# Attention and a gated feed-forward on one core: the eight PSUM banks become one pool, buffers are placed by the plan, and the order is another

## The chip, the cores and the metric

One core of a Trainium2 chip runs the whole program. TensorE (PE) multiplies matrices out of SBUF into the eight banks of PSUM; VectorE (DVE), ScalarE (ACT) and GpSimd (POOL) do the rest, the first two out of SBUF and PSUM, the third out of SBUF alone in this kernel; SyncE (SP) issues the DMAs. The metric is the device time of one execution in microseconds, the median over the runs. A measurement of this kernel tells a difference of about 0.2% from none.

## What is computed

```
# q, k, v: (8 batches, 8 heads, 576 positions, 64); attention inside chunks of 64 positions
scores = scale * q_c @ k_c.T                    # per batch, head and chunk: 64 x 64
attn   = exp(scores - max) ; attn /= sum + 1e-9
x      = attn @ v_c  -> (8, 576, 512)           # heads side by side
h      = relu(x @ w_in)                         # 512 -> 1024
c[s]   = w0*h[s-1] + w1*h[s] + w2*h[s+1]        # depthwise, along the positions of a batch
out    = (h * sigmoid(c)) @ w_out               # 1024 -> 512
```

q, k and v are fp32. The three weights arrive in 64-bit words, which the kernel reads as pairs of 32-bit words and turns into fp32 itself.

## The kernel before

**Tiles and blocks.** The 4608 positions of all batches are 36 tiles of 128 (two chunks of 64 each). Four tiles are one unit `u` (9 units of 512 columns). For each tile: q and k are loaded and turned (`t_pe` on PE and a copy out of PSUM for tiles 0 to 8, `t_dve` on DVE from tile 9), `scores` on PE (16 products of 64x64 per head half, 32 in all), the softmax (`s_max`, `s_sub` on DVE, `s_exp` on ACT, `s_sum`, `s_eps`, `s_rec` on DVE, a scaling on POOL), the transpose of the weights (`p_pe` on PE for tiles 0 to 11, later a swap by DMA and `p_dve`), `attn_v` on PE, and the result split into a high and a low part (`x_hi` on ACT, `x_lo` on DVE). From tile 4 on two tiles go through scores and attention together.

**The feed-forward.** Every product with a weight is three matmuls (high by high, high by low, low by high). `mm1` makes one block of 128 of the 1024 features for one unit: 12 matmuls of 512 columns (for unit 0 two halves of 256, since its first two tiles are there earlier). ACT and DVE then work on the block in its PSUM bank: `h_relu`, copies of the rim columns, `c_mid`, `c_left`, `c_right`, `c_sig`, `c_mul`; the bank is held from `mm1` to the end of `c_mul`. `g_hi` (on ACT, DVE or POOL) and `g_lo` (POOL) split the result. `mm2` then sums 8 features x 3 matmuls for one output tile of 128 rows into one bank, `o_copy` takes it out (ACT or DVE) and `o_store` writes it.

**The weights.** Each piece is loaded (`w_load`), scaled on ACT (`w_scale`), put together on DVE (`w_shift`, `w_words`) and split (`w_hi`, `w_left`, on the engine that the table `moved_` names).

**PSUM before.** Six banks (`banks`, index chosen by the plan) serve everything but scores and attention; these two share one pair of banks, `sx`: each tile uses one half (256 columns) of both banks, so two tiles fill the pair. Scores of the next two tiles can't begin before `x_lo` of the last attention has read the pair, and attention not before `s_sub` of the last scores.

**SBUF before.** Working buffers come from pools that rotate by the order of allocation (`rawv`, `work`, `work3`).

**The order.** All work is cut into 1990 steps, each with its engine, a planned cost, what it waits for, and what buffers it takes and frees. A list, `order_`, gives the sequence that was found by a search outside the kernel; `moved_` gives the engine of the steps that have a choice. The kernel runs through `order_` once, keeps a clock for each engine, hands out banks (each time the one that is free longest), and then emits the steps in order of their planned start. Each engine keeps that order. Where the plan leaves PE idle in its first 110 us, filler matmuls on the identity are put in (L978 of 512 columns, L981 of 128); their result isn't used.

Of the kernel before, what the change touches and what calls it, by code (L numbers as in the profile page):

```python
# [18 lines left out]
def attn_ffn(ctx: ExitStack, tc: tile.TileContext, q, k, v, w_in, conv_w, w_out, out):  # L19
# [4 lines left out]
    P = 128  # L24
# [14 lines left out]
    NB = 6  # L39
# [4 lines left out]
    rawv = ctx.enter_context(tc.tile_pool(name="rawv", bufs=3))  # L44
    work = ctx.enter_context(tc.tile_pool(name="work", bufs=2))
    work3 = ctx.enter_context(tc.tile_pool(name="work3", bufs=3))
    sb_w, sb_g = ExitStack(), ExitStack()
    ps_s = ctx.enter_context(tc.tile_pool(name="ps_s", bufs=1, space=PSUM))
    ps_b = ctx.enter_context(tc.tile_pool(name="ps_b", bufs=1, space=PSUM))
# [12 lines left out]

    sx = [ps_s.tile([P, 2, 512], F32, name=f"sx{i}_ps") for i in range(4 - NB // 2)]
    banks = [None] * NB
# [57 lines left out]
    def load_group(j):  # L122

        if not groups:
            sb_w.close()
            groups["raw"] = ctx.enter_context(tc.tile_pool(name="raw", bufs=2, side="right"))
        groups[j] = groups["raw"].tile([P, 2, G, 4 * TG, 32], F32, name="qk")
# [17 lines left out]
    def load_v(st, t):  # L145
# [6 lines left out]
        r = rawv.tile([P, G, 2, D], F32, name="v")  # L152
# [5 lines left out]
        if t == 0:  # L158
            st["u"] = work3.tile([P, UN], F32, name="c")[:, 0:G * D].rearrange("p (g d) -> p g d", d=D)
            heads(st["u"], 0, 1, slice(1, H, 2), C)  # L160
        else:
            st["u"] = st["last"]["w"]
# [18 lines left out]
    def turned(st):  # L181
        if 0 not in st:
            st["qk"] = work.tile([P, 2, G, 2 * C], F32, name="qkT")
            st[0], st[1] = st["qk"][:, 0], st["qk"][:, 1]
        return st["qk"]
# [15 lines left out]
    def sx_half(i):  # L201
        return sx[i // 2][:, :, G * C * (i % 2):G * C * (i % 2) + G * C]

    def sx_bank(i, u):
        return sx_half(i)[:, u, :]

    def scores(st):

        qT, kT = st[0], st[1]
        for g in range(G):  # L210
            for s in range(2):
                for hp in range(2):
                    d0 = 64 * hp
                    nc.tensor.matmul(  # L214
                        sx_bank(st["s"], hp if st["t"] >= TP else hp ^ s)[C * s:C * s + C, C * g:C * g + C],
# [5 lines left out]
    def s_max(st):  # L221
        st["m"] = work.tile([P, 2, G], F32, name="m")
        sv = sx_half(st["s"]).rearrange("p u (g j) -> p u g j", j=C)
        nc.vector.tensor_reduce(out=st["m"], in_=sv, op=ALU.max, axis=AX.X)  # L224

    def s_sub(st):
        st["e"] = work.tile([P, H, C], F32, name="e")
        nc.vector.tensor_tensor(
            out=st["e"].rearrange("p (g u) j -> p u g j", u=2), in0=sx_half(st["s"]).rearrange("p u (g j) -> p u g j", j=C),
# [9 lines left out]
    def s_sum(st):  # L239
        st["z"] = work.tile([P, H], F32, name="z")  # L240
# [11 lines left out]
    def two(st, name):  # L252
        if name not in st["two"]:
            st["two"][name] = work3.tile([P, 2 * DM], F32, name="wt").rearrange("p (n b h j) -> p n b h j", n=2, b=2, h=H)
        return st["two"][name][:, st["n"]]
# [15 lines left out]
    def p_dve(st):  # L271
        st["pT"] = work.tile([P, G, P], F32, name="pT")
# [13 lines left out]
    def p_copy(st, copy=nc.scalar.copy):  # L286
        st["pT"] = work.tile([P, G, P], F32, name="pT")
# [5 lines left out]
    def attn_v(st):  # L293
        for g in range(G):
            for s in range(2):
                for hp in range(2):
                    j0, m, vt = C * s, hp, st["v"][:, :, hp, :]
                    if st["t"] < TP:
# [4 lines left out]
                        sx_bank(st["x"], s)[D * hp:D * hp + D, C * g:C * g + C],  # L303
# [17 lines left out]
    def x_src(st):  # L321
        return sx_half(st["x"]).rearrange("p s (g i) -> p g s i", i=C)
# [46 lines left out]
    def c_mid(st, u, f):  # L369
        i0, n = span(u)  # L370
        st["c"] = work3.tile([P, UN], F32, name="c")[:, 0:n]
# [99 lines left out]
    def o_copy(st):  # L471
        st["os"] = work.tile([P, DM], F32, name="os")
        nc.scalar.mul(out=st["os"], in_=banks[st["o"]], mul=0.5)

    def o_copy_v(st):
        st["os"] = work.tile([P, DM], F32, name="os")
# [12 lines left out]
    def w_load(st, src):  # L489
        np_, n, m2 = src.shape  # L490
        if "at" not in st and "wslot" not in st:
            t = work.tile([P, DM], F32, name="os")
# [8 lines left out]
    def w_tile(st, name):  # L501
        n = st["L"].shape[1] * st["L"].shape[2]
        if name == "wt":
            st["w"] = work3.tile([P, 2 * DM], F32, name="wt")
# [81 lines left out]
    room = {"slot": 2, "wslot": 2, "sx": 8 - NB, "bk": NB, "grp": 2, "v": 3, "qkT": 2, "m": 2, "e": 2, "z": 2, "pT": 2, "c": 3, "wt": 3, "os": 2, "rc": 2}  # L586
    slot_users, place_users, row_users = [], {}, []

    def split(key, t_load, src, hi=None, lo=None, half=False, at=None):
# [4 lines left out]
        ld = step("SP", 0.57, t_load, w_load, (st, src), take=["os"] if small else [("wslot", st)] if at is None else [], lag=0.1 if small else 2.7 if at == 0 else 1.5 if half else 3.0)  # L594
        if small:
            s1 = step("DVE", a, key, w_mask, (st,), [ld], take=["wt"], port=True)
# [3 lines left out]
            s5 = step("DVE", b, key + 0.03, w_sign, (st,), [s2, s4], free=["os"], port=True)  # L600
# [3 lines left out]
            s8 = step("PE", 0.2, key + 0.04, c_pe, (st,), [s8], take=[("bk", st, "ct")], free=["wt"])  # L604
            return step("DVE", 0.2, key + 0.04, c_copy, (st,), [s8], free=[("bk", "ct")])
        s1 = step("ACT", c + 0.09, key, w_scale, (st,), [ld], take=["wt"])
        s2 = step("DVE", a, key, w_shift, (st,), [s1], port=True)
        s4 = step("DVE", b, key + 0.01, w_words, (st,), [s2], free=["wslot"] if at is None else [], port=True)
# [419 lines left out]
```

## Time and profile before

| | |
|---|---|
| median of 3 runs | 486.23 us (485.35 to 486.42) |
| profiled execution: its time / its span | 483.82 us / 482.0 us |
| PE busy | 469.7 us (97%) |
| DVE / ACT / POOL busy | 347.7 (72%) / 231.3 (48%) / 191.4 us (40%) |
| granted clock of PE, mean | 0.998 |
| HBM read / written | 36.72 / 9.44 MB |

The span runs from the first to the last instruction; the 1.8 us between the span and the execution's own time lie around it. The profiled execution is 2.4 us shorter than the median of the three runs. A matmul's busy time includes its pipeline, so matmuls in a row overlap in the records; what a stretch takes is read from starts.

### The profile page before, as it was taken

What the parts mean: (1) busy time and instruction counts of PE and PEld (TensorE: products, weight loads), DVE (VectorE), ACT (ScalarE), POOL (GpSimd) and SP (SyncE); (2) the same over time, 40 slices, a digit from 0 to 9 for tenths busy, and PEclk for the clock granted to TensorE, in tenths of its full rate; (3) what the DMA queues carried; (4) which work ended last, traced back from release to release, by engine and by line L of the source; (5) the groups of instructions that cost most, each with busy time, mean ns of one, the idle gap of its engine ahead of it and who ended that gap; (6) DMA issues with size and microseconds to landing.
All of it is one profiled execution on the core that took longest, in us unless ns stands there. A gap on an engine that the chain in (4) does not pass through costs nothing.

```text
span 482.0 us, 11324 instructions
## 1 busy us (share of the span) xinstructions
PE 469.7 (97%) x4401; PEld 386.2 (80%) x4401; DVE 347.7 (72%) x612; ACT 231.3 (48%) x531; POOL 191.4 (40%) x257
## 2 busy tenths in 40 slices
PE   8889999999999999999999999999999999999996
PEld 6789878887888888888888888888788888888885
DVE  3899997778758883989389748785779488624640
ACT  3547873555454742473267336651544165423430
POOL 1435546143333561355145423543255415502330
PEclk9999999999999999999999999999999999999999
DMA  7999945334567454336464624236642014000102
GB/s 213 234 303 248 274 68 95 67 51 78 96 149 176 97 99 116 49 72 134 110 139 76 123 67 106 48 56 158 117 92 46 22 63 114 3 22 22 45 22 87
DMA packets 180457, 50.06 MB, mean 104 GB/s; under 512 B 164508, under 2 KB 172724, under 8 KB 180404
## 3 DMA queue, kind: packets, MB, share of 16 engines
q1 hardware_dynamic: 180404, 49.34, 45.2%
q8 instruction: 34, 0.56, 0.5%
q14 instruction: 19, 0.16, 0.1%
HBM read 36.72 MB, written 9.44 MB: 96 GB/s over the span
## 4 chain that ended last, share of the span: by engine, by line
PE 75%; SPq 12%; DVE 7%; issue 2%; DMA 2%; POOL 1%; ACT 1%; POOLq 0%; ACTq 0%; DVEq 0%
PE b_ps L468 36%; PE b_ps L336 31%; SPq L141 10%; PE sx_ps L302 3%; PE sx_ps L214 3%; DMA r<-in_k 2%; DVE wt L520 1%; DVE wt L515 1%; SPq L111 1%; PE b_ps L174 1%; DVE x_l L328 1%; PE b_ps L283 1%; SPq L150 1%; DVE c L377 1%; DVE m L224 0%
## 5 line engine op out<-in xcount | busy, mean ns | idle before, releaser
L416 POOL TENSOR_TENSOR g_l<-c,g_h 128x510 fp32r<-128x510 f32 (+1 forms) x80 | 79.6, 1003 | 105.2 <-DVE g_h L405 43.4
L468 PE MATMUL b_ps<-wo_h,g_h 128*128 128x512 f32 x288 | 114.9, 399 | 1.0 <-ACT qkT L192 1.0
L468 PE MATMUL b_ps<-wo_h,g_l 128*128 128x512 f32 x288 | 112.3, 390 | 0.0
L468 PE MATMUL b_ps<-wo_l,g_h 128*128 128x512 f32 x288 | 112.2, 390 | 0.0
L336 PE MATMUL b_ps<-x_h,wi_h 128*128 128x512 f32 (+1 forms) x320 | 80.7, 374 | 0.0
L377 DVE SCALAR_TENSOR_TENSOR c<-b_ps,cw,c 128x510 f32<-128x510 f32 x72 | 53.1, 740 | 36.8 <-ACT rim L362 17.5
L336 PE MATMUL b_ps<-x_l,wi_h 128*128 128x512 f32 (+1 forms) x320 | 78.8, 368 | 0.0
L336 PE MATMUL b_ps<-x_h,wi_l 128*128 128x512 f32 (+1 forms) x320 | 78.7, 368 | 0.0
L343 ACT ACTIVATE b_ps<-b_ps 128x512 f32<-128x512 f32 x62 | 36.2, 584 | 73.2 <-PE b_ps L336 73.0
L336 PEld LDWEIGHTS b_ps<-x_l,wi_h 128*128 128x128 f32 x320 | 56.8, 188 | 10.2
L336 PEld LDWEIGHTS b_ps<-x_h,wi_l 128*128 128x128 f32 x320 | 56.9, 188 | 10.0
L468 PEld LDWEIGHTS b_ps<-wo_h,g_h 128*128 128x128 f32 x288 | 54.0, 188 | 13.4 <-issue 1.3
L336 PEld LDWEIGHTS b_ps<-x_h,wi_h 128*128 128x128 f32 x320 | 55.9, 188 | 10.5 <-DVE c L393 0.2
L468 PEld LDWEIGHTS b_ps<-wo_h,g_l 128*128 128x128 f32 x288 | 54.1, 188 | 11.5
L468 PEld LDWEIGHTS b_ps<-wo_l,g_h 128*128 128x128 f32 x288 | 54.1, 188 | 10.3
L389 ACT ACTIVATE c<-c 128x510 f32<-128x510 f32 (+1 forms) x72 | 45.4, 634 | 31.8 <-DVE c L383 31.3
L372 ACT ACTIVATE c<-b_ps,cw 128x510 f32<-128x510 f32 (+1 forms) x72 | 49.7, 692 | 21.6 <-DVE b_ps L347 15.6
L393 DVE SCALAR_TENSOR_TENSOR c<-c,b_ps 128x510 f32<-128x510 f32 (+1 forms) x72 | 48.1, 671 | 10.2 <-ACT c L389 6.6
L383 DVE SCALAR_TENSOR_TENSOR c<-b_ps,cw,c 128x510 f32<-128x510 f32 (+1 forms) x72 | 53.4, 744 | 2.2 <-ACT rim L362 0.7
L405 POOL CAST g_h<-c 128x510 fp32r<-128x510 f32 x25 | 15.3, 611 | 69.0 <-DVE c L393 68.2
L259 POOL TENSOR_TENSOR wt<-wt,z 128x512 f32<-128x512 f32 x24 | 25.2, 1052 | 42.1 <-DVE z L250 21.3
L199 DVE STREAM_TRANSPOSE qkT<-qk 128x512 f32<-128x512 f32 x54 | 36.2, 687 | 6.6 <-DMA qk<-in_k 4.2
(87 smaller groups left out, 518.8 us busy)
## 6 DMA issues: line engine op xcount, KB each, us to landing
out<-os SPq DMA_DIRECT2D x35, 256.0 KB, 2.3
v<-in_v SPq DMA_DIRECT2D x21, 256.0 KB, 3.6
qk<-in_k SPq DMA_DIRECT2D x96, 48.0 KB, 2.4
qk<-in_q SPq DMA_DIRECT2D x96, 48.0 KB, 2.4
w<-in_moe_w_out SPq DMA_DIRECT2D x4, 1024.0 KB, 5.3
v<-in_v SPq DMA_DIRECT2D x27, 128.0 KB, 3.1
wt<-wt SPq DMA_DIRECT2D x48, 64.0 KB, 2.0
qk<-in_k SPq DMA_DIRECT2D x96, 24.0 KB, 1.9
```

The source lines that it names most:

```text
L141: nc.sync.dma_start(out=groups[j][p0:p0 + 32, i, g, n0:n0 + 2 * n, :], in_=(q, k)[i][b, 2 * g + hp, t0:t0 + C * n, 32 * a:32 * a + 32].rea ...
L199: nc.vector.transpose(out=turned(st)[:, i].rearrange("p g (n i) -> p g n i", i=32), in_=groups[t // TG][:, i, :, 4 * (t % TG):4 * (t % TG) ...
L259: nc.gpsimd.tensor_tensor(out=two(st, "to"), in0=two(st, "of"), in1=z, op=ALU.mult)
L336: nc.tensor.matmul(banks[st["h"]][:, c0:c1], lhsT=wt[:, f // 2, kt, P * (f % 2):P * (f % 2) + P], rhs=xt[:, u % 2, kt, c0:c1], start=n == ...
L343: nc.scalar.activation(out=h, in_=h, func=AF.Relu)
L372: nc.scalar.mul(out=st["c"], in_=banks[st["h"]][:, i0:i0 + n], mul=cw[:, FT + f:FT + f + 1])
L377: nc.vector.scalar_tensor_tensor(out=c[:, a:n], in0=banks[st["h"]][:, i0 + a - 1:i0 + n - 1], scalar=cw[:, f:f + 1], in1=c[:, a:n], op0=AL ...
L383: nc.vector.scalar_tensor_tensor(out=st["c"], in0=banks[st["h"]][:, i0 + 1:i0 + 1 + n], scalar=cw[:, 2 * FT + f:2 * FT + f + 1], in1=st["c ...
L389: nc.scalar.activation(out=st["c"], in_=st["c"], func=AF.Tanh, scale=0.5)
L393: nc.vector.scalar_tensor_tensor(out=st["c"], in0=st["c"], scalar=1.0, in1=banks[st["h"]][:, i0:i0 + n], op0=ALU.add, op1=ALU.mult)
L416: nc.gpsimd.tensor_tensor(out=g_l[:, f, gs], in0=st["c"][:, cs], in1=g_h[:, f, gs].bitcast(F32), op=ALU.subtract)
L468: nc.tensor.matmul(banks[st["o"]], lhsT=gt[:, f, o:o + P], rhs=wt[:, f, :], start=f == 0 and n == 0, stop=f == FT - 1 and n == 2)
```

## The change

- The pair `sx` is gone. One PSUM tile `b_ps` of eight banks serves all. Scores or attention of two tiles take two neighbouring banks when they begin and give them back when the last `s_sub` or `x_lo` has read them. `bank_for` chooses: among banks that are free in time, those with the fewest open neighbours.
- The rotating pools are replaced by fixed tiles (`spots`); the plan says which of them a step uses. Numbers of buffers are the same (`room`).
- Steps that read one bank on ACT and DVE (the rim copies and `c_left`/`c_right`, and now each visit by itself) are kept apart in the plan by a tag (`bank=`).
- `order_` and `moved_` are new, from a search under two models of the loads.

```
-    NB = 6
+    NB = 8
...
-    sx = [ps_s.tile([P, 2, 512], F32, name=f"sx{i}_ps") for i in range(4 - NB // 2)]
-    banks = [None] * NB
+    room = {"slot": 2, "wslot": 2, "bk": NB, "grp": 2, "v": 3, "qkT": 2, "m": 2, "e": 2, "z": 2, "pT": 2, "c": 3, "wt": 3, "os": 2, "rc": 2}
...
+    all_banks = ps_s.tile([P, NB, 512], F32, name="b_ps")
+    banks = [all_banks[:, i] for i in range(NB)]
...
+    def half(st, name):
+
+        b, o = st["both"][name, 0], G * C * st["half"]
+        return all_banks[:, b:b + 2, o:o + G * C]
...
-                 take=[("sx", st_, "s") for st_ in sts], free=["qkT"] * len(tiles), bank="sx")
+                 take=[("bk", both, ("s", u)) for u in range(2)], free=[("qkT", st_["t"]) for st_ in sts], bank=tag)
...
-                 take=[("sx", st_, "x") for st_ in sts], bank="sx",
+                 take=[("bk", both, ("x", u)) for u in range(2)], bank=tag + 1, behind=[before.get("attn")],
...
-    moved_ = {15: 1, 16: 0, 21: 1, 27: 1, 28: 0, 33: 1, 39: 0, 45: 1, 51: 1, 58: 0, 64: 0, 69: 1, 73: 0, 94: 0,
+    moved_ = {16: 0, 22: 0, 27: 1, 34: 0, 40: 0, 45: 1, 46: 0, 51: 1, 63: 1, 70: 0, 73: 0, 94: 0, 113: 0, 132: 0,
...
+    bank_free = [0.0] * NB
+
+    def bank_for(t, n, late_):
+
+        best = None
+        for b in range(NB + 1 - n):
+            if any(x is None for x in bank_free[b:b + n]):
+                continue
+            since = max(bank_free[b:b + n])
+            open_ = (b > 0 and bank_free[b - 1] is not None) + (b + n < NB and bank_free[b + n] is not None)
+            rank = (0, open_, since if n == 1 else 0.0) if since + late_ <= t else (1, since, 0.0)
+            if best is None or rank < best[0]:
+                best = rank, b
+        return best[1]
```

What the new order moves, at three places. First PE just ahead of the first `mm2`, before (L336 is `mm1`, L214 scores, L179 the turning of q and k, L468 `mm2`, L978 and L981 fillers):

```order
L981 MATMUL b_ps<-ident 128x128 x3
L214 MATMUL sx_ps<-qkT 64x64 x32
L336 MATMUL b_ps<-x_h,wi_h 128x256 x4
L336 MATMUL b_ps<-x_l,wi_h 128x256 x4
L336 MATMUL b_ps<-x_h,wi_l 128x256 x4
L978 MATMUL b_ps<-ident 128x512
L981 MATMUL b_ps<-ident 128x128 x6
L179 MATMUL b_ps<-ident,qk_107 128x128 x8
L468 MATMUL b_ps<-wo_h,g_h 128x512
```

and the same place now, from the scores of tiles 6 and 7 (L220) on; L289 is `p_pe`, L342 `mm1`:

```order
L220 MATMUL b_ps<-qkT_72 64x64 x16
L220 MATMUL b_ps<-qkT_73 64x64 x16
L289 MATMUL b_ps<-ident,e_76 128x128 x4
L342 MATMUL b_ps<-x_h,wi_h 128x256 x4
L342 MATMUL b_ps<-x_l,wi_h 128x256 x4
L342 MATMUL b_ps<-x_h,wi_l 128x256 x4
```

The fillers on either side of these scores are gone, and the scores stand before the attention of tiles 4 and 5 instead of behind it. After the first load PE has 20 fillers of 128 columns and one of 512 before, 6 and one now. All of unit 0's `mm1` now stands ahead of the first `mm2`; before, 2 of its 16 halves stood behind. Ahead of the first `mm1` of unit 1 stand 18 steps of `mm2` (3 matmuls each) before and 6 now.

Second PE in the long even part, before: attention (L302) and, further on, scores (L214) each stand alone between products of the feed-forward:

```order
L336 MATMUL b_ps<-x_h,wi_h 128x512 x4
L336 MATMUL b_ps<-x_l,wi_h 128x512 x4
L336 MATMUL b_ps<-x_h,wi_l 128x512 x4
L302 MATMUL sx_ps<-pT,v 64x64 x32
L468 MATMUL b_ps<-wo_h,g_h 128x512
```

and now attention (L308) with the scores (L220) of other tiles right behind it:

```order
L342 MATMUL b_ps<-x_h,wi_l 128x512 x4
L308 MATMUL b_ps<-pT_80,v_69 64x64 x16
L308 MATMUL b_ps<-pT_81,v_67 64x64 x16
L220 MATMUL b_ps<-qkT_72 64x64 x16
L220 MATMUL b_ps<-qkT_73 64x64 x16
L474 MATMUL b_ps<-wo_h,g_h 128x512
```

Attention and scores of two tiles stand side by side at 9 places behind the first `mm1` of unit 1 now (4 times attention first, 5 times scores), at none before; the total of matmuls but for the fillers is the same.

Third the stores at the end of SP's queue, before (the last output tile is written in three pieces):

```order
L486 DMA out<-os 128x512 x10
L482 DMA out<-os 112x512
L483 DMA out<-os 15x512
L484 DMA out<-os 1x512
```

and now, where the tile in three pieces is the last but one:

```order
L488 DMA out<-os_71 112x512
L489 DMA out<-os_71 15x512
L490 DMA out<-os_71 1x512
L492 DMA out<-os_70 128x512
```

The last copy out of PSUM was on DVE and is on ACT now. On DVE, ahead of the eighth `c_mul` of unit 0, the new order has fewer instructions (110 for 120): no `g_hi` (6 before), no `p_copy` (1), 4 copies of turned q and k for 7, no cast of a weight (1), and one `w_left` of 512 columns more.

## Rows read from the trace of the kernel before

**Rows 1.** Busy time by stage: PE, its loads, DVE, ACT, POOL, PE's clock, DMA share.
```profile
0.00:5.24 5.24, 3.78 (x11) 2.27 (x11) 0.00 (x0) 1.49 (x2) 1.37 (x8) 1.00 0.45 126
5.24:62.45 57.21, 50.77 (x855) 45.55 (x856) 51.29 (x90) 35.86 (x66) 23.52 (x22) 1.00 0.98 258
62.45:71.49 9.04, 8.93 (x111) 7.22 (x111) 8.63 (x19) 6.29 (x12) 4.72 (x7) 1.00 0.43 70
71.49:478.00 406.51, 406.22 (x3432) 331.16 (x3425) 287.06 (x503) 187.71 (x454) 161.79 (x222) 1.00 0.39 82
478.00:482.00 4.00, 0.00 (x0) 0.00 (x0) 0.69 (x1) 0.00 (x0) 0.00 (x0) 0.76 0.37 131
```
**Rows 2.** PE's waits: line, releaser, us in total, times, longest.
```profile
PE b_ps L283 <- POOL e L276: 2.6, 4, 1.0
PE b_ps L174 <- DMA r<-in_k: 1.7, 2, 1.4
PE b_ps L468 <- ACT qkT L192: 1.0, 1, 1.0
PE sx_ps L214 <- DVE x_l L328: 0.9, 2, 0.7
```
**Rows 3.** Groups of PE between 5.24 and 71.49 us: the fillers.
```profile
L981 PE MATMUL b_ps<-ident 128*128 128x128 f32 x20 | 3.3, 278 | 0.0
L978 PE MATMUL b_ps<-ident 128*128 128x512 f32 x2 | 1.0, 590 | 0.0
```
**Rows 4.** PE in order of time around the first `mm2`: start, us.
```profile
55.02 0.49 PE L981 MATMUL b_ps<-ident 128*128 128x128 f32 x3
56.24 1.16 PE L214 MATMUL sx_ps<-qkT 64*64 64x64 f32 x64 [0.74 <-DVE x_l L328]
...
58.86 1.02 PE L978 MATMUL b_ps<-ident 128*128 128x512 f32 x2
59.72 0.82 PE L981 MATMUL b_ps<-ident 128*128 128x128 f32 x6
60.37 1.04 PE L179 MATMUL b_ps<-ident,qk 128*128 128x128 f32 x8
62.45 0.47 PE L468 MATMUL b_ps<-wo_h,g_h 128*128 128x512 f32 x1 [1.04 <-ACT qkT L192]
...
80.47 1.07 PE L336 MATMUL b_ps<-x_h,wi_h 128*128 128x512 f32 x4
```
**Rows 5.** The chain of waits, 159.98 to 174.40 us: start, us.
```profile
162.92 2.72 PE b_ps L336 x12
165.64 1.09 PE sx_ps L302 x64
166.73 2.95 PE b_ps L468 x12
169.68 1.09 PE sx_ps L214 x64
170.77 0.90 PE b_ps L468 x3
171.67 2.73 PE b_ps L336 x12
174.40 0.68 PE b_ps L468 x3
```
**Rows 6.** Groups of DVE over the span, by form.
```profile
L405 DVE CAST g_h<-c 128x127 fp32r<-128x127 f32 x4 | 1.8, 443 | 0.1
L405 DVE CAST g_h<-c 128x384 fp32r<-128x384 f32 x4 | 1.4, 348 | 0.0
L288 DVE COPY pT<-b_ps 128x512 f32<-128x512 f32 x3 | 2.0, 675 | 0.2 <-PE b_ps L283 0.2
L192 DVE COPY qkT<-b_ps 128x512 f32<-128x512 f32 x2 | 1.4, 683 | 0.0
L559 DVE CAST wi_h<-wt 128x1024 fp32r<-128x1024 f32 x1 | 0.7, 683 | 0.0
L524 DVE TENSOR_TENSOR wi_l<-wt,wi_h 128x512 fp32r<-128x512 f32 x2 | 1.4, 688 | 0.5 <-POOL wi_h L562 0.5
```
**Rows 7.** All engines at the end, in order of time: start, us.
```profile
477.38 0.60 ACT L473 ACTIVATE os<-b_ps 128x512 f32<-128x512 f32 x1 [6.83 <-PE b_ps L468]
477.58 0.39 PE L468 MATMUL b_ps<-wo_h,g_l 128*128 128x512 f32 x1
...
478.01 0.69 DVE L477 TENSOR_SCALAR os<-b_ps 128x512 f32<-128x512 f32 x1 [8.83 <-PE b_ps L468]
478.72 0.35 SPq L482 DMA_DIRECT2D out<-os  x1
479.13 0.45 SPq L483 DMA_DIRECT2D out<-os  x1
479.63 0.24 SPq L484 DMA_DIRECT2D out<-os  x1
```
**Rows 8.** The page's DMA issues: count, KB each, us to landing.
```profile
out<-os SPq DMA_DIRECT2D x35, 256.0 KB, 2.3
```

More of the change, by code (lines that the diff above doesn't have):

```diff
@@ L239, in s_sum @@
     def s_sum(st):
-        st["z"] = work.tile([P, H], F32, name="z")
+        st["z"] = spot("z", st["t"])
         if st["t"] >= TP:
@@ L491, in w_load @@
         if "at" not in st and "wslot" not in st:
-            t = work.tile([P, DM], F32, name="os")
+            t = spot("os", id(st))
         else:
@@ L630, in att @@
             ld = group(t // TG)
-            tt = [step("DVE", 0.7, key - 3, t_dve, (st, t, i), ld, take=["qkT"] * (1 - i)) for i in range(2)]
+            tt = [step("DVE", 0.7, key - 3, t_dve, (st, t, i), ld, take=[("qkT", t)] * (1 - i)) for i in range(2)]
             tt[1]["after"].append(tt[0])
             if t % TG == TG - 1:
-                tt[1]["free"] = ["grp"]
+                tt[1]["free"] = [("grp", t // TG)]
         parts = 1 if (2 * t) % NCK < NCK - 1 else 2
@@ L657, in attend @@
+        before["attn"] = s
         for st_ in sts:
             t = st_["t"]
-            a = step("ACT", 0.58, key + 1, x_hi, (st_, t), [s] + writes, bank="sx")
-            x_done[t] = step("DVE", 0.69, key + 1, x_lo, (st_, t), [a], free=[("sx", "x")], bank="sx")
-    def soft(st, s, key):
-        s = step("DVE", 0.69, key, s_max, (st,), [s], take=["m"], bank="sx")
-        s = step("DVE", 0.68, key, s_sub, (st,), [s], take=["e"], free=["m", ("sx", "s")], bank="sx")
+            a = step("ACT", 0.58, key + 1, x_hi, (st_, t), [s] + writes, bank=tag + 1)
+            x_done[t] = step("DVE", 0.69, key + 1, x_lo, (st_, t), [a], behind=[x_done[t - 1] if st_ is not sts[0] else None],
+                             free=[("bk", both, ("x", u)) for u in range(2)] if st_ is sts[-1] else [], bank=tag + 1)
@@ L665, in soft @@
+    def soft(st, s, key, tag, last):
+        s = step("DVE", 0.69, key, s_max, (st,), [s], take=[("m", st["t"])], bank=tag)
+        s = step("DVE", 0.68, key, s_sub, (st,), [s], take=[("e", st["t"])], behind=[st["both"].get("sub")],
+                 free=[("m", st["t"])] + [("bk", st["both"], ("s", u)) for u in range(2)] * last, bank=tag)
+        st["both"]["sub"] = s
         fold = st["t"] >= TP
         first = fold and not st["n"]
-        s = step("ACT", 0.63, key + 1, s_exp, (st,), [s], behind=[fold and st["two"].get("exp")], take=["wt"] * first, free=["e"] * fold)
+        s = step("ACT", 0.63, key + 1, s_exp, (st,), [s], behind=[fold and st["two"].get("exp")], take=[("wt", "of", st["t"])] * first, free=[("e", st["t"])] * fold)
@@ L668, in soft @@
         st.get("two", {})["exp"] = s
-        s = step("DVE", 0.68, key + 2, s_sum, (st,), [s], take=["z"])
+        s = step("DVE", 0.68, key + 2, s_sum, (st,), [s], take=[("z", st["t"])])
         s = step("DVE", 0.17, key + 2, s_eps, (st,), [s], port=True)
@@ L725, in rim_steps @@
         st = {}
-        s = step("POOL", 0.25, key, r_mid, (st, u), rims[u - 1] + rims[u], take=["rc"], port=True)
+        s = step("POOL", 0.25, key, r_mid, (st, u), rims[u - 1] + rims[u], take=[("rc", u)], port=True)
         for k in (0, 2):
@@ L961, in attn_ffn @@
         free_at[e] = t + cost - early[e]
-        for r in s["free"]:
-            r, name = (r, r) if isinstance(r, str) else r
-            b = s["args"][0][name] if r in ("slot", "wslot", "sx", "bk") else held[r][0]
-            held[r].remove(b)
-            free_buf[r].append((end[i], b))
+        for r, *who in s["free"]:
+            b = home_of[(r, *(id(x) if isinstance(x, dict) else x for x in who))]
             if r == "bk":
-                taken[b][-1][1] = end[i]
-    for i in range(NB):
-        banks[i] = ps_b.tile([P, 512], F32, name=f"b{i}_ps")
+                bank_free[b] = taken[b][-1][1] = end[i]
+            else:
+                free_buf[r].append((end[i], b))
     made = {}
```

168 lines of the change are left out of this document (92 added, 76 removed), and 211 rows, old and new, of tables (moved_, order_).

## Prediction, made before the changed kernel ran

> **What bounds the kernel now.** I read the busy times by stage first, because a PE that is busy 97% of the span says little while its fillers count as work. The table [rows 1] cuts the span at five places: the first real product (5.24 us), the first `mm2` (62.45), the end of the attention of tiles 6 and 7 (71.49) and the last product (478.0). Three things are to be seen. From 71.49 us on PE is busy for 406.2 of 406.5 us: this stretch ends when PE's work ends, and nothing but less work on PE shortens it. Between 5.24 and 62.45 PE is idle for 57.21 - 50.77 = 6.4 us, while DVE is busy for 51.3 of 57.2 us and the DMA engines 98%: this is a ramp in which DVE and the loads decide when PE gets work. The first 5.24 us wait for the first load, and the last 4.0 us are copy and store.
>
> Then the list of PE's waits [rows 2] says who ends the idle time in the ramp: POOL's scaling 2.6 us, loads 1.7, a copy on ACT 1.0, `x_lo` on DVE 0.9. Two of these are waits for PSUM as much as for data. In order of time [rows 4] the scores at 56.24 wait for `x_l`: that is the attention of the two tiles before, which has to leave the pair `sx` first. And the first `mm2` at 62.45 starts as soon as a copy of turned q or k has emptied a bank. The fillers that stand in the ramp are busy for 3.3 + 1.0 = 4.3 us [rows 3]. They fill time in which PE had nothing to do, so the ramp has 6.4 + 4.3 = 10.7 us without useful work.
>
> **The ramp (first term).** The new order keeps 6 of the 20 small fillers and the one large. At the mean of the group, 3.3 / 20 x 6 = 1.0, with 1.0 for the large one, 2.0 us stay. If all idle time went and no filler time turned into idle time, the ramp would be 10.7 - 2.0 = 8.7 us shorter. That is the upper end. Most of it isn't PSUM's to give: the loads that PE waits for stay, and DVE stays nearly full. What the pair and the banks hold is bounded by the place in [rows 4]: fillers 0.49 and wait 0.74 ahead of the scores, 60.37 - 58.86 = 1.51 of fillers ahead of the turning, and 1.04 of wait ahead of `mm2`, 3.8 us in all. With a pool of eight banks, scores needn't wait for `x_lo`, and `mm2` needn't wait for that copy.
>
> Does DVE let it happen? What it has to do ahead of the eighth `c_mul` of unit 0 shrinks, by the counts above and the durations of [rows 6]: 3 x 0.443 + 3 x 0.348 for `g_hi`, 0.675 for the copy, 3 x 0.683 for turned q and k, 0.683 for the cast, less 0.688 for the added `w_left`: 1.33 + 1.04 + 0.68 + 2.05 + 0.68 - 0.69 = 5.1 us. This work goes to ACT and POOL, which are busy for 35.9 and 23.5 of the 57.2 us [rows 1]; that idle time hides it. If ACT were as full as DVE, the casts would come back at once as later `g_lo` and later `mm2`. The order of POOL and ACT is new as well; I cost that at nothing for the same idle time.
>
> So DVE gains more (5.1) than the places of PSUM hold (3.8), but from its side the end of the ramp is later products' data, not the eighth `c_mul` alone, and the loads have a new order whose fit I can't see. In it the fourth tile's q and k come ahead of the first piece of weights, which should shorten the 1.7 us of waits for loads; but a whole piece of 1 MB is the first to be worked on, and DVE has its `w_shift` in front of the scores of tiles 2 and 3. These two I set against each other. I take 2.5 us, two thirds of 3.8; the bounds are 0 and 8.7.
>
> **Attention beside scores (second term).** In the even part the chain of waits [rows 5] shows what a visit to the 64x64 products costs beyond their own 1.09 us. Twelve `mm1` take 2.72 us. Between two visits, twelve `mm2` take 2.95. So 0.23 us go for leaving one visit and entering the next, that is for each visit. Where attention and scores follow one another directly, one leaving and one entering are saved: 9 places x 0.23 = 2.1 us. The trace of before has no such neighbours in the even part; scores directly behind attention could cost as much as `mm2` behind attention, and then the term is 0. The nearest row is the visit itself: 64 products of two tiles in 1.09 us, with no step where the second tile begins. I take 2.0, bounds 0 and 2.1.
>
> The Trainium skill, "TensorEngine Tiling (Array Packing)", section "Key Properties", says that a change of tiling mode drains TensorE while a change of tile within a mode doesn't. By that rule the 0.23 us is the drain, attention and scores share the 64x64 mode, and the sum has the full 2.1 us. No run shown so far has the neighbours that would prove it.
>
> **The end (third term).** Before, the last product starts at 477.58; DVE copies from 478.01 to 478.70, and SP issues three pieces until 479.63 + 0.24 = 479.87 [rows 7], so the last store leaves SP 1.15 us after the first piece. Now ACT copies, which takes 0.60 in the same rows for 0.69, and SP issues one store. By the issues of [rows 7] that saves 0.69 - 0.60 = 0.1 and up to 479.63 - 478.72 = 0.9 of issue time; but the whole tile lands after 2.3 us [rows 8], and the first small piece was nearly as large, so only part comes back. I take 0.4, bounds 0 and 1.0. The buffer of that last copy was stored from just before; between the products of the two tiles stand 5 steps of `mm2`, 5 x 0.68 = 3.4 us [rows 5], against 0.6 + 2.3 for copy and store, so it is free in time.
>
> **What costs nothing.** The fixed places for buffers have the same numbers of buffers as the pools. The plan's tags keep ACT and DVE apart on one bank as the chip's waits did before. Choosing banks happens when the program is built. The cover of all these is PE's full row from 71.49 us on: if a bank, a buffer or an operand came late there, it would show as a wait of PE, and there is one of 0.2 us before (0.9 in two waits, 0.74 of it in the ramp [rows 2]).
>
> **Sum.** 2.5 + 2.0 + 0.4 = 4.9 us off the profiled execution's 483.8, which is 478.9. That execution is 2.4 us under the median of the runs; off the median the same 4.9 us give 481.3.
>
> **Rivals.**
>
> *DVE and the loads keep the ramp as it is.* For it: DVE 90% and the DMA engines 98% busy there [rows 1], and idle time that PSUM did not cause. Against it: 5.1 us less on DVE. Only the second and third term are left: 486.2 - 2.4 = 483.8.
>
> *Nothing comes of it.* The ramp stays, attention beside scores costs a leaving and an entering like any other visit, and the end gives 0.4 or nothing: 486. For it, no row shows the neighbours.
>
> *The ramp gives much more.* Fillers and waits mostly go, since the loads and the first pieces of weights fit better too: 8.7 of the first term with 2.4 of the others is 11.1; half of the way from 2.5 to 8.7 gives 486.2 - 5.6 - 2.4 = 478.2.
>
> *Scores wait for two neighbours (the other side).* One pool for all means that a visit now competes with `mm1` and `mm2`, which hold banks for long: it needs two free banks side by side, and PE stands still in the fixed order until the slower is read out. Everything behind it on PE waits too, and PE has no spare time. The price of a wait of this kind is 0.74 us [rows 4]; at each of the 14 scores of tiles 8 to 35 it would be 10.4 us. It decides from 4.9 / 14 = 0.35 us for each score on; at 0.74 the time would be 486.2 - 4.9 + 10.4 = 491.7, at half of that 486.5. Against it: eight banks where six and a pair were, and PE's even part had hardly a wait with less freedom.
>
> *PE's clock falls in the ramp.* With 14 fillers fewer PE could stand idle longer in one piece. The clock is 1.00 in every stage up to 478 us and 0.76 after PE has stopped [rows 1], so idleness does lower it. Five microseconds of work at 1.2 in place of 2.4 GHz are 5 us lost, the whole gain: 486.2. Against it: the longest wait in the ramp is 1.4 us [rows 2], with the clock at 1.00. The Trainium skill, "TensorE: Matmul & The Clock Gate", section "Why this matters for your kernels", warns of idle gaps between bursts of matmuls, which bring back the lower clock; by that rule fewer fillers speak against the change, and the trace so far has gaps that it bore.
>
> **How the numbers follow.** Chances: forecast 0.52, ramp as it is 0.16, much more from the ramp 0.08, nothing comes of it (with the clock) 0.12, waits for two neighbours 0.12. About 0.2% is what a measurement of this kernel tells from no change, here 1 us. The first three cases are faster: 0.76. The fourth is the same: 0.12. The fifth is slower: 0.12. The likeliest time is 481.3, in its own case between 479.5 and 483. The range reaches up to 486.6, over the unchanged time, and down to 478.2, the better ramp; it leaves out the waits for two neighbours beyond half of the price and the rest of the better ramp.
>
> **What would show it.** Right: PE's idle time between its first real product and the first `mm1` of unit 1 at some 4 us for 6.4, fillers under 2 us busy, and that `mm1`, which starts at 80.47 before [rows 4] and now stands behind 6 steps of `mm2` instead of 18, starting near 80.5 - 12 x 0.68 - 2.5 = 69.8 us; `mm2` between an attention-scores pair and the next visit showing the same 0.23 us once for two visits; a last copy on ACT. Wrong: PE waiting from 75 us on for a reader of `b_ps` (`x_l`, `e` or `os`), which is the fifth case; a step of 0.2 us between attention and scores, the fourth; DVE full and PE's waits unchanged up to 62 us, the second; a granted clock under 1.00 in the ramp. What would make the forecast wrong without any of these is a load of the new order that comes late and holds all of DVE's queue.

## The result, and the profile after

The changed kernel takes 479.78 us (median of 4 runs, 478.41 to 481.11) against 486.25 for the kernel before beside it: ratio 0.9871, 95% interval 0.9832 to 0.9909. The forecast was 481.3, in a range of 478.2 to 486.6. Single times of either kernel spread over some 7 us, so the 0.2% of the section on the metric is too fine: the interval of this ratio is 0.8% wide. All runs of this study together give 486.4 for the kernel before (55 runs, 483.8 to 490.7) and 480.4 for the changed one (15 runs, 477.5 to 484.6), a gain of 6.0. One more run of the changed kernel, of 485.27 us, was in the slow state and is left out here and below. The profiled executions are both from the low end of their kernels: 483.82 and 478.63 us. What follows accounts for these 5.2 us.

First the changed kernel's table by stage, cut at the first real product, the first `mm2`, the first `mm1` of unit 1 and the last product; the columns are those of [rows 1].

```profile
5.29:59.90 54.61, 50.06 (x859) 45.83 (x859) 48.56 (x92) 39.35 (x71) 16.96 (x18) 1.00 0.97 269
59.90:69.09 9.19, 7.98 (x101) 6.21 (x100) 8.89 (x13) 7.45 (x17) 7.58 (x8) 1.00 0.39 66
69.09:473.00 403.91, 402.36 (x3423) 330.57 (x3421) 289.17 (x510) 184.64 (x448) 156.00 (x217) 1.00 0.39 83
473.00:476.90 3.90, 0.04 (x1) 0.00 (x0) 0.00 (x0) 0.60 (x1) 0.00 (x0) 0.89 0.38 134
```

Up to the first `mm2` PE is idle for 54.61 - 50.06 = 4.55 us, where it was 6.4 [rows 1]; from there to the first `mm1` of unit 1 another 9.19 - 7.98 = 1.21, in `p_pe` and the attention of tiles 6 and 7, where it was 0.1 up to 71.49 us. The fillers among PE's groups between 5.29 and 69.09 us:

```profile
L1019 PE MATMUL b_ps<-ident 128*128 128x128 f32 x7 | 1.3, 272 | 0.0
L1016 PE MATMUL b_ps<-ident 128*128 128x512 f32 x2 | 1.0, 590 | 0.0
```

That is 2.3 us of fillers for 4.3 [rows 3]; one of the seven small ones is the last of those ahead of the first product. PE in order of time around the first `mm2`, for [rows 4]:

```profile
51.28 1.16 PE L220 MATMUL b_ps<-qkT 64*64 64x64 f32 x64
...
55.83 1.16 PE L308 MATMUL b_ps<-pT,v 64*64 64x64 f32 x64
...
59.41 0.64 PE L342 MATMUL b_ps<-x_h,wi_l 128*128 128x256 f32 x4
59.90 0.40 PE L474 MATMUL b_ps<-wo_h,g_h 128*128 128x512 f32 x1
...
69.09 1.08 PE L342 MATMUL b_ps<-x_h,wi_h 128*128 128x512 f32 x4
```

The scores of tiles 6 and 7 start at 51.28 and wait for nothing, the attention of tiles 4 and 5 follows at 55.83, and the first `mm2` waits for no copy. `mm1` of unit 1 starts at 69.09. Before, it started at 80.47 behind 12 more steps of `mm2`: 80.47 - 12 x 0.68 = 72.31. The ramp is **3.2 us** shorter.

The list of PE's waits (line, releaser, us, times, longest), for [rows 2]:

```profile
PE b_ps L289 <- POOL e L282: 1.7, 4, 0.6
PE b_ps L1016 <- POOL ident masks.py:199: 1.4, 1, 1.4
PE b_ps L220 <- issue: 1.1, 1, 1.1
PE b_ps L220 <- ACT os L479: 0.8, 1, 0.8
```

The last of them is new: scores wait for a copy of an output tile. The chain of waits where scores and attention now stand side by side, for [rows 5]:

```profile
123.99 1.09 PE b_ps L220 x64
125.08 0.93 PE b_ps L308 x64
126.02 3.11 PE b_ps L474 x12
129.12 2.72 PE b_ps L342 x12
```

The second visit takes 0.93 us and follows without a gap. From 123.99 to 129.12 two visits and twelve `mm2` take 5.13 us; by [rows 5] apart they were 1.09 + 1.09 + 2.95 and another 0.23, which is 5.36. The saving is 0.23 us at this place. But the twelve `mm2` behind the pair are 0.16 us slower here than the 2.95 of [rows 5]; six of the nine pairs have no such loss, the one at 338.06 us among them:

```profile
338.06 1.09 PE b_ps L220 x64
339.15 0.93 PE b_ps L308 x64
340.08 2.95 PE b_ps L342 x12
```

Two visits and twelve products take 4.97 us, 0.39 less than apart: 0.23 for one leaving and one entering, and 0.16 in the second visit itself. The whole even part, reckoned with those 12 steps, is 477.97 - 80.47 + 8.16 = 405.66 before and 473.05 - 69.09 = 403.96 after: **1.7 us**. The end, in order of time, for [rows 7]:

```profile
472.66 0.39 PE L474 MATMUL b_ps<-wo_h,g_l 128*128 128x512 f32 x1
473.13 0.60 ACT L479 ACTIVATE os<-b_ps 128x512 f32<-128x512 f32 x1 [2.80 <-PE b_ps L474]
473.75 0.36 SPq L492 DMA_DIRECT2D out<-os  x1
```

From the end of the last product to the span's end it is 3.81 us where it was 4.07: **0.3 us**. Sum: 3.2 + 1.7 + 0.3 = 5.2.

### The profile page after: what moved, and what is told of

Read it like the earlier page. It is cut to its first block, busy times and chain, and to the rows that moved or that the text cites. A ratio compares the mean times of both kernels' runs of the same rounds, so it can differ in the third digit from the quotient of the medians.

```text
span 476.9 us, 11252 instructions
## 1 busy us (share of the span) xinstructions
PE 464.4 (97%) x4389; PEld 385.2 (81%) x4389; DVE 346.6 (73%) x613; ACT 233.5 (49%) x537; POOL 181.9 (38%) x250
## 2 busy tenths in 40 slices
DMA packets 180457, 50.06 MB, mean 105 GB/s; under 512 B 164508, under 2 KB 172724, under 8 KB 180404
## 4 chain that ended last, share of the span: by engine, by line
PE 80%; DVE 7%; ACT 4%; DMA 3%; POOL 2%; issue 2%; SPq 1%; DVEq 0%; POOLq 0%; ACTq 0%
PE b_ps L474 39%; PE b_ps L342 34%; PE b_ps L308 3%; PE b_ps L220 3%; DMA w<-in_moe_w_in 2%; SPq L117 1%; DVE wt L526 1%; DVE c L389 1%; PE b_ps L289 1%; DVE c L383 1%; ACT x_h L331 1%; DVE x_l L334 1%; DVE c L399 1%; DVE qkT L206 1%; ACT wt L517 1%
## 5 line engine op out<-in xcount | busy, mean ns | idle before, releaser
L474 PE MATMUL b_ps<-wo_h,g_h 128*128 128x512 f32 x288 | 113.6, 394 | 0.0
L342 PE MATMUL b_ps<-x_h,wi_h 128*128 128x512 f32 (+1 forms) x320 | 80.6, 374 | 0.4 <-DVE x_l L334 0.3
L342 PE MATMUL b_ps<-x_l,wi_h 128*128 128x512 f32 (+1 forms) x320 | 78.8, 368 | 0.0
L342 PE MATMUL b_ps<-x_h,wi_l 128*128 128x512 f32 (+1 forms) x320 | 78.7, 368 | 0.0
L342 PEld LDWEIGHTS b_ps<-x_l,wi_h 128*128 128x128 f32 x320 | 56.9, 188 | 10.2
L342 PEld LDWEIGHTS b_ps<-x_h,wi_l 128*128 128x128 f32 x320 | 56.9, 189 | 10.0
L342 PEld LDWEIGHTS b_ps<-x_h,wi_h 128*128 128x128 f32 x320 | 55.9, 188 | 11.1 <-ACT c L395 0.7
L349 ACT ACTIVATE b_ps<-b_ps 128x512 f32<-128x512 f32 x57 | 33.4, 587 | 64.0 <-PE b_ps L342 63.7
L331 ACT CAST x_h<-b_ps 128x512 fp32r<-128x512 f32 x36 | 20.4, 591 | 27.5 <-PE b_ps L308 26.1
```

Of the source, the lines that this page charges most:

```text
L331: nc.scalar.copy(out=x_view(t, x_h), in_=x_src(st))
L342: nc.tensor.matmul(banks[st["h"]][:, c0:c1], lhsT=wt[:, f // 2, kt, P * (f % 2):P * (f % 2) + P], rhs=xt[:, u % 2, kt, c0:c1], start=n == ...
L349: nc.scalar.activation(out=h, in_=h, func=AF.Relu)
L474: nc.tensor.matmul(banks[st["o"]], lhsT=gt[:, f, o:o + P], rhs=wt[:, f, :], start=f == 0 and n == 0, stop=f == FT - 1 and n == 2)
```

## The experiments

Each kernel was profiled once and timed beside the kernel before; eight are edits of the changed kernel, e1 takes the lists of before, e8 edits the kernel before, a0 and e11 are the changed kernel again. "First `mm1`" is the start of unit 1's first `mm1`, "even part" goes from there to the end of the last product, "stops" is PE's listed waits behind 75 us. Empty fields have no like to compare with (e1 and e8 have 18 steps of `mm2` ahead of that `mm1`). In e1, e2, e5 and e10 a step whose buffers aren't free when its turn comes is put off, which changes the order too: 105, 425, 34 and 72 of the 1990 steps.

| kernel | median us | ratio to before (95%) | first `mm1` | even part | stops |
|---|---|---|---|---|---|
| a0 changed, again | 479.98 | 0.9864 (0.9814 to 0.9915) | 68.79 | 405.68 | 2.9 |
| e1 old order | 500.55 | 1.0281 (1.0237 to 1.0325) | | | |
| e2 one pair | 552.79 | 1.1369 (1.1314 to 1.1424) | 81.17 | | |
| e3 split | 482.69 | 0.9916 (0.9887 to 0.9945) | 68.53 | 408.48 | 2.4 |
| e4 two stores | 480.08 | 0.9874 (0.9832 to 0.9917) | 68.86 | 404.24 | 1.1 |
| e5 DVE loaded | 486.49 | 0.9994 (0.9962 to 1.0025) | 73.16 | 407.14 | 4.1 |
| e6 no filler | 481.33 | 0.9886 (0.9835 to 0.9937) | 69.57 | 407.81 | 3.9 |
| e7 no burst | 479.50 | 0.9865 (0.9824 to 0.9907) | 69.28 | 404.99 | 2.7 |
| e8 before, relieved | 486.74 | 1.0007 (0.9978 to 1.0035) | 82.09 | | |
| e9 five stores | 478.39 | 0.9843 (0.9801 to 0.9884) | 68.08 | 402.14 | 0.3 |
| e10 pair in ramp | 492.61 | 1.0135 (1.0098 to 1.0172) | 76.94 | 409.82 | 5.1 |
| e11 changed, beside e8 to e10 | 481.09 | 0.9899 (0.9850 to 0.9949) | 68.78 | 406.03 | 3.5 |

**a0, e11: the changed kernel again.** No edit.

> The changed kernel as it is, beside the others on one chip. Theory (two levels): single times of the kernel before and of this one each stand at one of two levels some 2.5 us apart, with mean granted clocks of about 0.996 and 0.999 to 1.000; like for like the change is worth 5.1 us (before 483.8 and 486.3, after 478.5 and 481.0). Rival (a real spread of waits): times lie anywhere between and the clock doesn't go with them.

> The changed kernel as it is, beside the other three on one chip, for what they are compared with. Its single times should lie between 477.5 and 482.5 us, and its profile should show PE stopped ahead of the scores at 208 us for 0.8 to 3 us behind the copy that waits for a store.

The theory of two levels fell: the times lie anywhere between 477.5 and 484.6, two of them above the 482.5 expected of e11. The longest have a lower mean clock (484.57 at 0.993), but it doesn't sort the rest (477.48 at 0.998, 481.09 at 1.000). The first `mm1` is within 0.3 us in three profiles (69.09, 68.79, 68.78); the even part varies from 403.96 to 406.03, and the stops with it, from 1.5 to 3.5. Without its stops it is 402.5 to 402.8 in all three. So 2 us of the spread are in those stops, and e4 and e9 go after them; where the rest of the 7 us is, no profile shows.

**e3: is the gain of neighbours real?**

```
+    pe = [i for i in order_ if steps[i]["eng"] == "PE"]
+    for n in range(1, len(pe) - 1):
+        if n > pe.index(place[id(mm1_of[1, 0])]) and {steps[i]["fn"] for i in pe[n - 1:n + 1]} == {scores_of, attn_of}:
+            order_.remove(pe[n + 1])
+            order_.insert(order_.index(pe[n]), pe[n + 1])
```

> The changed kernel with one product of the feed-forward put between attention and scores at the nine places where they stand side by side. Theory (each visit of its own costs the turn in and out once more, 0.23 us): the even part is 9 x 0.23 = 2.1 us longer, and the time 2.1 us above the changed kernel at the same clock. Rival (the turn is hidden or the gain came from elsewhere): under 0.5 us.

The median is 2.7 us above a0 on the same chip (the intervals of the two ratios overlap narrowly), the even part without its stops 406.1 against 402.5 to 402.8. The chain at the place shown above:

```profile
123.44 1.09 PE b_ps L220 x64
124.53 0.90 PE b_ps L474 x3
125.43 1.16 PE b_ps L308 x64
...
126.61 0.59 ACT x_h L331
...
127.24 2.29 PE b_ps L474 x9
```

Three `mm2` between the visits take 0.90, which are 0.68 [rows 5] and 0.22 of leaving and entering, and the attention, 1.16 to the end of its last product, is no longer the short second visit. The theory holds, but its price was too low: without stops the nine places cost 3.3 to 3.6 us and not 2.1; nine times the 0.39 of a clean pair are 3.5. New stops came with the edit (here 0.65 us for `x_h`), but they are already taken out of these figures.

**e1, e2: order and banks apart, over the whole program.** e1 has the lists of before in the changed kernel; e2 keeps the new lists and confines the banks, from tile 4 on to the pair of before. The loop that puts steps off, and the banks of e2:

```
-    for i in order_:
+    for i in feasible():
...
+    def places(wide, s):
+        if not wide:
+            return range(6)
+        return range(NB - 1) if s["args"][0][0]["t"] < 4 else range(6, 7)
```

> The eight-bank pool and the planned buffers, but the order and the engine table of the kernel before (a step whose buffer is not free yet when its turn comes is put off until it is). Theory (the order is what pays): the same as before, 486.2 +- 1.0, with the ramp up to unit 1 and the turns between attention and scores as they were. Rival (the banks pay by themselves): PE waits less for readers of the pair in the ramp, first mm1 of unit 1 at 70 to 71 us in place of 72.3, and 484 or less.

> The new order and engine table, but visits of two tiles may only use banks 6 and 7, and work of one bank only banks 0 to 5, as before; PE steps whose banks are not free are put off. Theory (the pool is needed for attention beside scores and for the scores of tiles 6 and 7 ahead of attention, the rest is order): the even part gives back its 2.0 us, the ramp some 1 us, so 3 us slower than the changed kernel like for like. Rival (the pool is what pays): all 5 us are lost, 486. Third: nothing is lost, within 0.5 us of the changed kernel.

Both are far slower than either theory said, so neither number is the price of the pool or of the order alone. A list that was searched for one set of rules is a bad list under another. What they show is that this order and these banks are one design; what a new search with the old banks would have given was not tried. e8 and e10 ask the same of the ramp alone.

**e5, e8: is it the relief of DVE?** e5 puts nine pieces of unit 0's work back on DVE; e8 takes the same nine off it in the kernel before, with its order, its six banks and its pair.

```
+    moved_.update({178: 0, 204: 0, 211: 0, 222: 0, 233: 0, 267: 0, 269: 0, 273: 0, 311: 0})
```

```
+    for i in (204, 211, 267, 269, 273, 311):
+        del moved_[i]
+    moved_.update({178: 1, 222: 1, 233: 1})
```

> The changed kernel with nine pieces of work of the ramp back on DVE as in the kernel before (four copies of turned q and k, one relu, four g_hi of unit 0), some 5 us more on DVE ahead of unit 1; steps whose buffer is not free yet are put off. Theory (relief of DVE carries part of the ramp's 3.2 us): first mm1 of unit 1 at 70.5 to 73 us in place of 69.1, the time 1.5 to 4 us up. Rival (the ramp is set by PE, the loads and the banks): under 0.5 us.

> The kernel before, its order and its six banks and pair, with the nine pieces of work of the ramp taken off DVE that the changed kernel has on ACT and POOL (four copies of turned q and k, one relu, four g_hi of unit 0). Theory (DVE's load alone sets the ramp): first mm1 of unit 1 some 2 to 3 us earlier than 80.47 us, and the time 2 to 3 us below the kernel before. Rival (banks and order are needed to use the room): the ramp within 0.7 us of before, and the time within 1 us.

e5 loses the ramp: first `mm1` at 73.16, 4.1 us later, and the whole gain of the change is gone (ratio 0.9994). That is more than the 1.5 to 4 us expected; the even part is 1.1 to 3.2 us longer as well, with one stop of 2.1 us for `x_h`. Its table by stage has a lower granted clock in the ramp, 0.96 over 42.51 us, which is at most 1.7 us of the 4.1:

```profile
20.00:62.51 42.51, 38.55 (x585) 35.99 (x582) 40.88 (x74) 29.77 (x54) 13.91 (x13) 0.96 0.91 258
```

e8 gains nothing (first `mm1` at 82.09 for 80.47), although DVE is 4.1 us less busy than in [rows 1]. The same stretch, and PE's waits there:

```profile
5.24:62.45 57.21, 50.87 (x857) 45.65 (x856) 47.20 (x84) 35.91 (x66) 23.38 (x21) 1.00 0.95 257
```

```profile
PE b_ps L174 <- DMA r<-in_k: 2.0, 3, 1.5
PE sx_ps L302 <- DMA v<-in_v: 1.8, 2, 1.4
PE b_ps L283 <- POOL e L276: 1.7, 3, 1.0
PE b_ps L468 <- ACT qkT L192: 1.1, 1, 1.1
PE sx_ps L214 <- DVE x_l L328: 0.7, 1, 0.7
```

The two waits for PSUM stand there as before, 1.1 for the copy ahead of `mm2` and 0.7 for `x_l` ahead of the scores, and the loads of v are a new one of 1.8 us; taken off as a whole, they would leave that `mm1` within 0.2 us of before. Relief of DVE is needed by the new order, and is worth nothing alone.

**e10: is it the banks?** As in e2, but only until PE's planned clock reaches 70 us.

```
+        if free_at["PE"] >= 70.0:
+            return range(NB - wide)
+        if not wide:
+            return range(6)
+        return range(6, 7) if s["args"][0][0]["t"] >= 4 else range(7)
```

> The changed kernel, its order and engine table, but for the first 70 us visits of two tiles may only use banks 6 and 7 and work of one bank only banks 0 to 5; behind that all eight are free as in the changed kernel. A step whose bank is not free when its turn comes is put off. Theory (the ramp's 3.2 us need the eight banks): first mm1 of unit 1 at 72 us or later in place of 69.1, 3 us or more lost. Rival (the relief of DVE and the order do it): under 1 us lost.

The first `mm1` starts at 76.94, 7.9 us later than in the first profile of the changed kernel and 8.2 later than in e11. Among PE's waits up to there:

```profile
PE b_ps L186 <- ACT qkT L199: 1.1, 2, 0.6
...
PE b_ps L342 <- DVE c L399: 0.7, 1, 0.7
PE b_ps L186 <- ACT rim L359: 0.6, 1, 0.6
PE b_ps L186 <- DVE c L399: 0.6, 1, 0.6
```

These are waits for banks: `mm1` and the turning of q and k for the readers of unit 0's blocks and of earlier turnings. They fit the changed kernel's own plan, in which work of one bank holds seven or eight banks at once at some places before 70 us. The 7.9 us bound the price from above, since 72 steps were put off and the order wasn't searched again for six banks; the even part, which has all eight, is 3.8 us longer than e11's too.

**e6, e7: do the fillers hold the clock?** e6 leaves out the fillers behind the first load, e7 starts the count late (`pe_free, until_ = 5.0, 110.0`), so that only three small ones stand ahead of it.

```
-        if steps[i]["eng"] == "PE" and begin[i] <= until_:
+        if steps[i]["eng"] == "PE" and begin[i] <= until_ and pe_free < 5.0:
```

> The changed kernel without its seven fillers behind the first load (their result is used by nothing). Theory (they stand in holes): within 0.5 us. Rival (they hold the clock): the granted clock falls in the ramp and the time is over 1 us up.

> The changed kernel with 3 fillers of 128 columns ahead of the first load in place of one of 512 and 10 of 128 (their result is used by nothing). Theory (PE must have worked before the first turning of q and k to have the high clock there): the granted clock falls below 0.99 in the first 30 us and the ramp is 1 to 4 us longer. Rival (PE waits for the loads anyway until 20 us): within 0.5 us.

First `mm1` at 69.57 and 69.28, 0.2 to 0.8 us later than in the three profiles of the changed kernel: fillers are worth no more than that in the ramp. e6's median is 1.4 us above a0's, with intervals that overlap. The granted clock is listed as 1.00 in every stage of both ramps, but its first stretch hides something. The first 32 records of the turning, in the changed kernel and in e7:

```profile
5.29 2.05 PE L181 MATMUL b_ps<-ident,r 128*64 128x128 f32 x32
```

```profile
5.22 3.68 PE L181 MATMUL b_ps<-ident,r 128*64 128x128 f32 x32 [2.96 <-DMA r<-in_k]
```

The same records take 1.6 us more in e7, behind three fillers and 2.96 us of waiting: that is what e7's theory expected of the clock, though the column doesn't show it. (In [rows 1], too, the column's 1.00 is no guide up to 5 us: the two records of the large filler take 2.07 us there and 1.02 at 58.86 [rows 4].) The 1.6 us are won back by 20 us: the next turning starts at 19.51 in the changed kernel, behind a stop and a wait for a load, and at 19.88 in e7, behind neither.

Both profiles caught the stop ahead of the scores at 208 us, 2.85 us long in e6 and 1.59 in e7. Busy time and clock of e6 (first the stop, then what follows it):

```profile
208.53:211.38 2.85, 0.00 (x1) 0.00 (x0) 1.30 (x2) 1.30 (x4) 2.37 (x3) 1.00 0.97 279
211.38:215.00 3.62, 3.62 (x68) 3.09 (x69) 2.97 (x5) 1.21 (x3) 3.33 (x4) 0.67 0.92 187
```

and of e7:

```profile
208.38:209.97 1.59, 0.01 (x1) 0.01 (x1) 0.43 (x1) 1.30 (x4) 1.59 (x3) 1.00 1.01 240
209.97:214.00 4.03, 4.03 (x75) 3.20 (x76) 3.39 (x6) 1.28 (x4) 3.34 (x4) 1.00 1.02 232
```

After 2.85 us without a product the granted clock is 0.67, a mean between its two levels of 2.4 GHz (1.00) and 1.2 GHz (0.50), and the twelve `mm1` behind it take 4.53 us (212.47 to 217.00) in place of 2.72: the stop costs 1.8 us more than its own length. After 1.59 us in e7 it stays at 1.00. The Trainium skill, "TensorE: Matmul & The Clock Gate", section "Why this matters for your kernels", warns of just such gaps; in e6 the trace agrees. In the ramps of e6 and of the changed kernel, with gaps of up to 1.5 us, the clock doesn't fall; in e5's, with one of 1.9 us, it does.

**e4, e9: the stop at 208 us.** In the changed kernel, in order of time (SP's issues, ACT's copies of output tiles, the scores):

```profile
201.75 2.51 SPq L275 DMA_DIRECT2D wt<-wt  x4
204.35 1.02 SPq L492 DMA_DIRECT2D out<-os  x2
...
206.64 0.60 ACT L479 ACTIVATE os<-b_ps 128x512 f32<-128x512 f32 x1 [1.00 <-DMA out<-os]
...
206.99 0.32 PE L220 MATMUL b_ps<-qkT 64*64 64x64 f32 x2
207.48 0.60 ACT L479 ACTIVATE os<-b_ps 128x512 f32<-128x512 f32 x1 [0.19 <-DMA out<-os]
...
208.13 1.08 PE L220 MATMUL b_ps<-qkT 64*64 64x64 f32 x57 [0.82 <-ACT os L479]
```

Two stores, ready long before (the last copy for them ends at 183.7), are issued behind loads and the swap. The copies on ACT wait for them to land, since both `os` buffers are taken. The scores have one free bank (one product, two records, runs) and wait for its neighbour, which the copy still holds. The edits put stores ahead of what stands before them; e4 has only the pair at 204 us:

```
+    for i, ahead in ((244, 525), (254, 525), (447, 935), (690, 935), (901, 1187)):
+        order_.remove(i)
+        order_.insert(order_.index(ahead), i)
```

> The changed kernel with the two stores of output tiles that it issues at 204 us put ahead of the swap of the attention weights in SP's queue (one place of four DMAs). Theory (the changed kernel has a new wait of its own: the two stores stand behind the loads and the swap, land at 206 to 207 us, the two copies on ACT that need their buffers wait 1.0 to 1.7 us, the bank comes free late, and the scores at 208 us wait 0.8 to 1.5 us): that stop of PE goes, and the time is 0.8 to 1.5 us below the changed kernel. Rival (the swap is late then): the attention at 212 us waits in place of the scores, and nothing is won.

> The changed kernel with five stores of output tiles earlier in SP's queue: two each at 122 and 204 us and one at 258 us, each put ahead of loads or of a swap that stand in front of it. Theory (the stops of PE at 127, 208 and 262 us, 0.8 to 3.5 us together from run to run, come from stores that land late): they are gone, and the time is 1 to 2 us below the changed kernel beside it, with less spread. Rival (the loads that are pushed back, or chance elsewhere, take it): within 0.5 us of the changed kernel.

In e4 the stop at that place is gone:

```profile
201.49 0.86 SPq L492 DMA_DIRECT2D out<-os  x2
202.45 2.52 SPq L275 DMA_DIRECT2D wt<-wt  x4
...
205.55 0.59 ACT L479 ACTIVATE os<-b_ps 128x512 f32<-128x512 f32 x1
...
206.99 1.16 PE L220 MATMUL b_ps<-qkT 64*64 64x64 f32 x64
```

but another of the kind, at 262 us, is 0.64 long there, and the median doesn't differ from a0's. With all five stores the even part is 402.14, below all three profiles of the changed kernel, and its one listed stop is 0.34 us for `x_l`. e9 has the lowest median of the study: 478.39 against 481.09 for e11 beside it. The intervals of their ratios overlap (0.9801 to 0.9884, 0.9850 to 0.9949), so the size of this gain, 1.6 us by a0's median and 2.7 by e11's, isn't settled; that the stops are gone is shown in its one profile. Its single times still spread over 5.9 us (475.8 to 481.7), so the smaller spread that was expected is not shown.

## Why the prediction was right, point by point

- **The ramp**, 2.5 forecast, 3.2 measured (3.5 in the profiles of a0 and e11). The places named for PSUM behaved as said: no wait of the scores for `x_lo`, none of `mm2` for the copy, and `mm1` at 69.09 for 69.8. PE's idle time from its first product to that `mm1` fell less than said: 4.55 + 1.21 = 5.8 us, where "some 4" were forecast, and fillers are 2.3 us for "under 2". The ramp is shorter all the same, since 2.0 us less of fillers and 0.7 us less of idle time add up to 2.7 of the 3.2; the other 0.5 isn't assigned. This order needs both the banks (e10) and the relief of DVE (e5), and relief alone does nothing (e8). The prediction had treated DVE's 5.1 us as what *lets* PSUM's 3.8 happen; the runs fit that. It had kept 1.3 of the 3.8 back for the loads; 0.7 of that came. How much of the ramp a new search with the old banks would have given stays open, and so does what the fixed buffers and the tags did by themselves.
- **A load that holds DVE**, which the last sentence of the prediction feared, came in small: DVE stands idle from 16.4 to 18.7 us until ACT has the first weights. What it cost isn't shown. PE's stop of 1.1 us in the scores there ends at 17.55, before DVE works again, and the profile names no releaser for it; in e11 it is missing, PE waits 1.3 us for k instead, and the first `mm1` is 0.3 us earlier.
- **Attention beside scores**, 2.0 forecast, 1.7 measured in the first pair of profiles. That it comes so near is luck: two larger sizes were off, and they nearly cancel. The mechanism is right, but a pair saves 0.39 us where nothing else stops PE, not 0.23: the prediction took the second visit at the full 1.09 us, and it takes 0.93. Nine pairs make 3.5; without its stops (1.5 us, 0.2 before) the even part is 3.0 shorter, and e3 takes 3.3 to 3.6 back. The stops, which the sum put at nothing, take 1.3 to 3.3 away again. In the profiles of a0 and e11 the even part is 405.68 and 406.03 for 405.66 before, so there nothing is left of this term. The Trainium skill, "TensorEngine Tiling (Array Packing)", section "Key Properties", says that a change of mode drains TensorE and a change of tile doesn't; the second visit's 0.93 us without a gap agrees.
- **The end**, 0.4 forecast, 0.3 measured: the last store leaves SP 0.83 us sooner after the last product than before, but from there to the span's end it takes 2.7 us for 2.2; the store is a whole tile now and was one row.
- **Scores wait for two neighbours**, the rival with 0.12, is real at one of its fourteen places: 0.82, 1.53, 1.37, 2.85 and 1.59 us in the changed kernel's three profiles, e6 and e7. It is the wait for `os` that the prediction named as a sign of being wrong. At this one place it costs one to four times the 0.74 us of the rival; at the other thirteen it didn't come, but an attention at 262 us waits for such a copy too, 0.5 and 0.6 us in a0 and e11. The bank held is that of an `mm2`, but it is held so long by a late store behind its copy (e4).
- **The clock in the ramp** did not fall in the changed kernel (1.00), nor in e6, with still fewer fillers; e7 lost 1.6 us at its first products, which cost nothing in the end. It did fall in e5, with PE stopped for up to 1.9 us by POOL's scaling there, and in the even part behind some stops.
- **The median.** The forecast took 4.9 us off the median 486.23; the first pair of profiles differs by 5.2, the medians beside each other by 6.5 (4.4 to 8.2 by the interval), those over all runs by 6.0. Against the one profile of the kernel before, which is among its fastest executions, a0's profile gains 3.8 and e11's 3.4. So the total is sure to some 2 us, and that its terms add up to 5.2 in one pair is in part luck.

## What to carry to other kernels

A resource that is split by use costs twice: the wait for the other use, and the order that it forbids. Give it free together with a new order and a new share of work between engines: here each alone gave nothing or lost. And look in the queue of issues for stores that have long been ready: they cost nothing in the plan until their buffers are the last two, and then a late landing reaches TensorE through a copy and a bank.

## What was not expected of the hardware

A stop of TensorE in the middle of full work can be charged twice: 2.85 us in e6 left a clock of 0.67 over the next 3.6 us, 2.54 us in e10 one of 0.62 over 4 us, while 0.82 to 1.59 us in the changed kernel and e7 left it at 1.00. Length alone doesn't decide it. In e1 the clock is 0.50 from 227.5 to 230.8 us behind stops of 1.13 and 0.44 us, and in e2 it stays at 1.00 behind one of 2.94:

```profile
170.71:173.65 2.94, 0.00 (x1) 0.00 (x0) 2.90 (x9) 0.69 (x2) 0.60 (x2) 1.00 0.58 94
173.65:177.65 4.00, 3.99 (x17) 3.30 (x18) 2.64 (x5) 0.92 (x2) 2.64 (x3) 1.00 0.60 96
```

What else decides it is open. Eleven fillers ahead of the first load, in place of three, spared 1.6 us at the first products and were worth nothing that the time shows (e7 479.50, a0 479.98), as PE waits for loads up to 20 us anyway. And a visit of 64x64 products right behind another saves not only one leaving and one entering: it is itself 0.16 us shorter (0.93 for 1.09).
